# Causal score blocks in two column halves, filler products in TensorE's early gaps, and 224 slots per expert

## The chip, the core and the metric

The kernel runs on one core of one Trainium2 chip. The core has five engines with queues of their own: TensorE (PE in the views; its weight loads are listed apart as PEld), VectorE (DVE), ScalarE (ACT), GpSimd (POOL) and SyncE (SP), which here issues most DMAs. The metric is the device time of one execution in microseconds (us). Matrix products read SBUF and write PSUM, and whatever goes into another product is first copied out of PSUM by ACT or DVE.

## The reference

Inputs q, k, v, a_re, a_im have the shape (4, 8, 768, 48): batch, heads, steps, width. The first half is a linear recurrence with a complex decay, of which the real part is read out:

```python
mag = np.sqrt(a_re * a_re + a_im * a_im)
scale = np.minimum(mag, 0.999) / (mag + 1e-06)
a_re_n, a_im_n = (a_re * scale, a_im * scale)
for t in range(S):
    new_re = ar * S_re - ai * S_im
    new_im = ar * S_im + ai * S_re
    kv = np.einsum('bhd,bhe->bhde', k[:, :, t], v[:, :, t])
    S_re, S_im = (new_re + kv, new_im)
    y[:, :, t] = np.einsum('bhd,bhde->bhe', q[:, :, t], S_re)
```

The result, as 3,072 rows of 384, goes through a mixture of eight experts (widths 384, 1024, 384). A row is computed only if `x @ w_skip > 0`; it goes to the expert with the largest gate logit, and the others are passed through:

```python
for e in range(E):
    mask = e_idx == e
    h = np.maximum(xc[mask] @ w1[e], 0.0)
    y[mask] = gate_w[mask, None] * (h @ w2[e])
out[do_compute] = xc + y
```

With the reference's own inputs 1,500 rows are computed, and the eight experts receive 180, 186, 199, 177, 182, 217, 175 and 184 of them.

## The kernel before, in words

**Units.** Time is cut into six chunks of 128 steps. A unit `u` is one chunk of one batch (all 8 heads), 24 units in all; `c, b = divmod(u, 4)`.

**Attention.** For each unit ACT and DVE make the decay of each step (`gates`), in groups of units because the logarithm, exponential and trigonometric tables of ACT are loaded in turn; running sums over the steps are products with a triangle (`pt`, `pl`). `ready` scales q and k, turns them (`w`), transposes both on TensorE (`tp`, four heads at a time) and copies the transposes to SBUF (`wT`, on ACT). `unit` then makes the scores of four heads at a time (`pa`, line 451): per head one product with 128 key steps as weights (k transposed, 96 rows by 128 columns) and 128 query steps as moving columns. DVE multiplies them with a triangle of ones (`at`, line 457), so that only keys not later than the query remain. `ps` and `T` carry the state, `py` is scores times v plus the state's part. In `py` the weights have 64 columns, and even and odd heads write the lower and the upper 64 partitions of PSUM. `px` makes the gate logits; `route` gives each row a slot of its expert, and an indirect DMA on POOL writes the row there (`xs`).

**Experts.** Each expert has CAP = 256 slots, as two tiles of 128. Numbers are split into a high and a low part in the one-pass format fp32r. Per expert: fetch of the slots (`xg`), six transposes (`tx`, line 862; for the first expert, products `ga` with one-hot rows instead), the split (`xh`, `xl`), 8 groups of 9 products with 128 weight columns and 256 moving columns (`ph`, line 886), relu and split (`hh`, `hl`), 2 by 24 products of 384 moving columns (`po`, lines 907 to 909), scale and add (`og`), and an indirect DMA to the output. If an expert had more rows than slots, a slow branch (`dense`) would follow at the end.

**The order.** `Plan.order` writes out the order of the instructions on each engine ahead of the run: it plays the program through with a cost for each operation (the `us` of `add`), and takes, of what could start within NEAR of the earliest, what has the smallest due time (`at`). The engines then follow that fixed order, and wait where an input is late. The constants at the top (STARTS, LEADS, PULL and others) set the groups and the due times; SHARE names copies that DVE makes in place of ACT.

An f32 product shows in the trace as two instructions (two passes), a transpose and an fp32r product as one.

Of the kernel before, what the change touches and what calls it, by code (L numbers as in the profile page):

```python
# [31 lines left out]
ROOMS = dict(ain=6, tr=5, U=6, cs=2, e=5, qk=4, w0=2, w1=2, wT0=2, wT1=2, vt=3, at=2, st=2, yT=2, row=4, G=1, raw=2, raw2=4,  # L32
             tp=2, pa=2, y=1, g=1, c=2, xa=3, mpt=2, mph=3, mpo=3, xg=2, xh=2, hh=2, og=2)
LEADS = {0: 5.96, 1: 3.48, 2: 2.07, 3: 1.5, 4: 2.5, 5: 2.37, 6: 2.26, 7: 2.47}
SHARE = lambda u: ((0, 1), (1, 1)) if u < 0 else ()
# [7 lines left out]
CAP = 256  # L43
# [4 lines left out]
class Plan:  # L48
# [4 lines left out]

    def __init__(self, rooms):
        self.rooms, self.ops, self.rel = rooms, {}, {}

    def add(self, key, eng, us, at, need=(), take=(), free=()):
        def put(fn):
            need_ = list(need)
            if (key[0], key[1] - 1) + key[2:] in self.ops and key[0][:2] not in ("rt", "ro", "re"):  # L60
                need_.append((None, (key[0], key[1] - 1) + key[2:]))
            self.ops[key] = (eng, us, at, need_, list(take), fn)
            for x in free:
                self.rel.setdefault(x, []).append(key)
        return put

    def order(self):
        end, free, held, out = {}, dict.fromkeys("PAVGS", 0.0), {"xa": [("xa", "z")]}, []
        pipe, warm = 0.0, [-9.0, 0.0]
# [32 lines left out]
        while todo:  # L102
            can = {}
            for key in todo:
                r, e = ready(key), self.ops[key][0][0]
                if r is not None:
                    can.setdefault(e, []).append((max(r, free[e]), self.ops[key][2], key))
# [5 lines left out]
            eng, us, at, need, take, fn = self.ops[key]  # L113
            if len(eng) > 1:
# [3 lines left out]
            else:  # L118
                if e == "P":
                    if s - warm[0] > 3.0:  # L120
                        warm[1] = 0.0
                    if s < COLD or warm[1] < 4.0:
# [12 lines left out]
        assert len(out) == len(self.ops), sorted((k for k in self.ops if k not in end), key=str)[:9]  # L135
# [4 lines left out]
class Kern:  # L140
# [12 lines left out]
    def consts(self, ctx):  # L153
# [57 lines left out]
    def late(self, k):  # L211
# [18 lines left out]
        nc.sync.dma_start(self.xs[k * r:(k + 1) * r].rearrange("(p n) d -> p (n d)", n=B), self.z)  # L230
# [18 lines left out]
    def gates(self, u, k, t, end):  # L249
# [60 lines left out]
        @add(("pt", u), "P", 0.75, t1, [("on" if c else "atan", u)], take=[("c", "pt", u)])  # L310
# [34 lines left out]
        @add(("pl", u), "P", 0.72, t2, [("U", u), ("pt", end - 1)], take=[("c", "pl", u)], free=[("U", u)])  # L345
# [43 lines left out]
    def ready(self, u, t):  # L389
# [15 lines left out]
        for k in range(2):  # L405
# [6 lines left out]
            for hh in range(2):  # L412
                @add(("tp", u, k, hh), "P", 0.455, t, [("w", u, k)], take=[("tp", u, k, hh)], free=[(f"w{k}", u)])
# [19 lines left out]
    def unit(self, u):  # L433
# [7 lines left out]
        @add(("lv", u), "S1", 1.0, t - PULL, take=[("vt", u)])  # L441
        def _():
            vt = X["vt", u] = self.vts[u % len(self.vts)]
            nc.sync.dma_start(vt[:, :, 0:D], self.rows(self.v, c, b))

        for hh in range(2):
            @add(("pa", u, hh), "P", 0.91, t, [("wT", u, k, hh) for k in range(2)], take=[("pa", u, hh)], free=[("wT1", u)])
            def _(hh=hh):
                pa = X["pa", u, hh] = self.ps_at.tile([128, 4, C], F32, name=f"pa_{nm}_{hh}", tag="pa")
                for h in range(hh * 4, hh * 4 + 4):  # L450
                    PE.matmul(pa[:, h % 4], X["wT", u, 1][:, h], X["wT", u, 0][:, h], start=True, stop=True)  # L451

            @add(("at", u, hh), "V", 0.686, t, [("pa", u, hh)], take=[("at", u)], free=[("pa", u, hh)])
            def _(hh=hh):
                if ("at", u) not in X:
                    X["at", u] = self.un.tile([128, H, C], F32, name=f"at_{nm}", tag="at", bufs=self.rooms["at"])
                V.tensor_tensor(X["at", u][:, hh * 4:hh * 4 + 4], X["pa", u, hh],  # L457
                                self.mask.rearrange("p (o t) -> p o t", o=1).to_broadcast([128, 4, C]), ALU.mult)
# [7 lines left out]
        if not late:  # L466
            @add(("ps", u), "P", 1.41, t, [("w", u, 1), ("lv", u)], take=[("g", "ps", u)], free=[("w1", u), ("vt", u)])
            def _():
                ps = X["ps", u] = self.ps_g.tile([96, H, D], F32, name=f"ps_{nm}", tag="g")
                for h in range(H):  # L470
                    PE.matmul(ps[:, h], X["w", u, 1][:, h].rearrange("p k d -> p (k d)"), X["vt", u][:, h, 0:D], start=True, stop=True)
# [9 lines left out]
        for hh in range(2):  # L481
            @add(("py", u, hh), "P", 0.97 if c else 0.48, t,
                 [("at", u, hh), ("lv", u)] + ([("Sb", u), ("wT", u, 0, hh)] if c else []),
                 take=[("y", u)], free=[("at", u), ("vt", u), ("wT0", u)] + [("st", u)] * (c > 0))
            def _(hh=hh):
# [3 lines left out]
                vt, at, qT, py = X["vt", u], X["at", u], X["wT", u, 0], X["py"]  # L489
# [14 lines left out]
        @add(("px", u), "P", 0.9, t, [("yT", u), ("wg", 0)], take=[bank], free=[("yT", u)])  # L504
# [43 lines left out]
    def early(self):  # L548
# [3 lines left out]
        nx = CAP // 128 * DM  # L552
        self.xe = m[:, 0:nx].rearrange("p (t d) -> p t d", d=DM)
        self.ohx = [o[:, b * CAP:(b + 1) * CAP] for b in range(B - 1)] + [m[:, nx:nx + CAP]]
        self.nc.sync.dma_start(self.xe, self.xs[0:CAP, 0:DM].rearrange("(t p) d -> p t d", p=128))
# [138 lines left out]
    def attention(self):  # L694
        with ExitStack() as ctx:
# [5 lines left out]
            self.ps_tp, self.ps_at = P("ps_tp", 2, space=PSUM), P("ps_at", 2, space=PSUM)  # L701
# [3 lines left out]
            self.vts = [pers.tile([128, H, 64], F32, name=f"vt{i}") for i in range(self.rooms["vt"])]  # L705
            self.sts = [pers.tile([96, H, 64], F32, name=f"st{i}") for i in range(self.rooms["st"])]
            for t in self.vts + self.sts:
# [109 lines left out]
    def experts(self):  # L817
# [6 lines left out]
        ks = lambda k: slice(k * 128, (k + 1) * 128)  # L824
        wTs = [("wT", u, k, hh) for k in range(2) for hh in range(2)]
        self.weights(1, n - 1.5, 0.15, [("w", u, 1)])

        def pts(e, t):
            if ("pts", e, t) not in X:
                X["pts", e, t] = self.pt_.tile([128, KD, 128], F32, name=f"pt_{e}_{t}", tag="pt")  # L830
            return X["pts", e, t]

        for b in (0, 1, 2, -1, 3):
# [4 lines left out]
            def _(b=b):  # L838
                for t in range(2):
                    for k in range(KD):  # L840
                        l, r = (self.xe[:, t, ks(k)], self.ident) if b < 0 else (self.xa[:, b, ks(k)], self.ohx[b][:, ks(t)])
                        PE.matmul(pts(0, t)[:, k], l, r, start=(b == 0 and k == 0), stop=True, skip_group_check=True)

        for e in range(E):
            te = T0 + TE * e

            @add(("xg", e), "S1", 1.1, te - 0.9, [("px", u)] + [(f"re{b}", 8) for b in range(B)], take=[("xg", e)])
            def _(e=e):
                xg = X["xg", e] = self.xp.tile([128, 2, XW], F32, name=f"xg_{e}", tag="xg")
                nc.sync.dma_start(xg, self.xs[e * CAP:(e + 1) * CAP].rearrange("(t p) d -> p t d", p=128))  # L850

            @add(("idx", e), "G", 0.2, te - 0.8, [("xg", e)])
            def _(e=e):
                X["idx", e] = self.xp.tile([128, 2], I32, name=f"idx_{e}", tag="idx")
                G.tensor_copy(X["idx", e], X["xg", e][:, :, DM])

            for t in range(2):
                if e:
                    @add(("tx", e, t), "P", 0.34, te - 0.8, [("xg", e)], take=[("mpt", e, t)])
                    def _(e=e, t=t):  # L860
                        for k in range(KD):
                            PE.transpose(pts(e, t)[:, k], X["xg", e][:, t, ks(k)], self.ident)

                @add(("xh", e, t), "A", 0.482, te - 0.75, [("tx", e, t) if e else ("ga", 3)], take=[("xh", e)])
                def _(e=e, t=t):
                    if ("xh", e) not in X:
                        X["xh", e], X["xl", e] = [self.xp.tile([128, KD, CAP], F32R, name=f"{a}_{e}", tag=a) for a in ("xh", "xl")]
                    A.copy(X["xh", e][:, :, ks(t)], pts(e, t))

                @add(("xl", e, t), "V", 0.553, te - 0.75, [("xh", e, t)], free=[("mpt", e, t)])  # L870
                def _(e=e, t=t):
                    V.tensor_tensor(X["xl", e][:, :, ks(t)], pts(e, t), X["xh", e][:, :, ks(t)], ALU.subtract)  # L872

            for j in range(NF):
                @add(("ph", e, j), "P", 1.08, te + j * 0.11,
# [12 lines left out]
                @add(("hh", e, j), "A", 0.381, te + j * 0.11, [("ph", e, j)], take=[("hh", e)])  # L888
# [5 lines left out]
                @add(("hl", e, j), "V", 0.418, te + j * 0.11, [("hh", e, j)], free=[("mph", e, j)])  # L894
# [3 lines left out]
            for t in range(2):  # L898
                for j in range(NF):
                    @add(("po", e, t, j), "P", 0.52, te + 0.95 + (t * NF + j) * 0.053,  # L900
                         [("hl", e, j), ("wl", e, KD + j // 2)] + [(None, ("po", e, t, j - 1))] * (j > 0) + [("px", u)] * (e == 0),
                         take=[("mpo", e, t)], free=[("hh", e)])
                    def _(e=e, t=t, j=j):
                        if j == 0:
                            X["po", e, t] = self.po_.tile([128, DM], F32, name=f"po_{e}_{t}", tag="po")
# [246 lines left out]
```

## Time and profile before

| | |
|---|---|
| median of 3 runs | 425.59 us (425.2 to 426.17) |
| the profiled execution | 426.13 us, its span 424.4 us |
| TensorE busy | 388.5 us (92%), 3,236 instructions |
| DVE busy | 319.3 us (75%) |
| ACT busy | 283.9 us (67%) |
| POOL busy | 56.6 us (13%) |
| DMA moved | 65.55 MB |
| mean granted TensorE clock | 0.979 |

The span goes from the first to the last instruction; the time of an execution has some 1.7 us more around it. A busy TensorE is not one at its peak: successive products overlap, so the distance between their starts is what one costs, not its duration. The granted clock is 1.00 at 2.4 GHz and 0.50 at 1.2 GHz.

### The profile page before, as it was taken

The page shows a single profiled execution, that of the slowest core. Times are in us where ns is not written, and L with a number is a line of the kernel's source. Part 1 is how long each engine was busy: PE and PEld are TensorE (multiplying, and loading weights), DVE is VectorE, ACT ScalarE, POOL GpSimd, SP SyncE. Part 2 cuts the span into 40 slices and gives each one's busy share as a digit, 9 for nine tenths or more (in the row PEclk, how much of TensorE's full clock was granted, in tenths as well). Part 3 has the DMA queues.
Part 4 walks back from the last instruction along what each step waited for, and adds up shares of the span by engine and source line. Part 5 has one row for each costly group of instructions (what it writes and reads, how often), then busy time and mean ns, then how long its engine had stood idle before and what let it go on. Part 6 is the DMA issues. An engine that isn't in the chain of part 4 may idle for free. (4 is left out here: it accounts for less than half of the span.)

```text
span 424.4 us, 8790 instructions
## 1 busy us (share of the span) xinstructions
PE 388.5 (92%) x3236; PEld 346.3 (82%) x3236; DVE 319.3 (75%) x722; ACT 283.9 (67%) x550; POOL 56.6 (13%) x94
## 2 busy tenths in 40 slices
PE   0569999999999999999999988899999999999992
PEld 0248689769868987997878977799999999999992
DVE  4469799979999978987997998877666676656220
ACT  5798998889798879849898654554454655446020
POOL 7000000014005003001300121101011010111101
PEclk9967999999999999999999999999999999999998
DMA  9999929986983892444423765586665766662001
GB/s 158 184 148 171 161 58 177 366 150 142 158 168 81 139 194 54 97 80 112 101 48 119 206 213 195 159 294 223 206 236 179 233 177 230 227 192 80 27 1 33
DMA packets 148049, 65.55 MB, mean 154 GB/s; under 512 B 129323, under 2 KB 143407, under 8 KB 148000
## 3 DMA queue, kind: packets, MB, share of 16 engines
q1 hardware_dynamic: 145440, 60.29, 60.7%
q0 software_dynamic: 2560, 4.63, 3.0%
q8 instruction: 28, 0.46, 0.5%
q14 instruction: 21, 0.17, 0.1%
HBM read 52.33 MB, written 15.77 MB: 160 GB/s over the span
## 5 line engine op out<-in xcount | busy, mean ns | idle before, releaser
L810 ACT CAST h<-r 128x768 fp32r<-128x768 f32 (+1 forms) x56 | 50.8, 926 | 38.5 <-issue 19.8
L815 DVE TENSOR_TENSOR l<-r,h 128x768 fp32r<-128x768 f32 (+1 forms) x56 | 58.9, 1069 | 7.8 <-ACT h L810 7.2
L558 POOL DMA_INDIRECT xs<-xa,sl x24 | 28.9, 1206 | 231.3 <-ACT tr L242 85.0
L418 PE MATMUL tp<-ident,w 128*96 128x128 f32 x384 | 55.0, 284 | 3.0 <-ACT wT L427 1.2
L886 PE MATMUL ph<-xh,h 128*128 128x256 f32 x192 | 54.6, 288 | 1.1 <-DVE hl L896 0.8
L418 PEld LDWEIGHTS tp<-ident,w 128*96 128x96 f32 x384 | 43.1, 131 | 14.6 <-issue 4.4
L427 ACT COPY wT<-tp 96x512 f32<-96x512 f32 x96 | 52.1, 580 | 2.8 <-PE tp L418 2.6
L886 PE MATMUL ph<-xh,l 128*128 128x256 f32 x192 | 53.6, 283 | 0.0
L451 PE MATMUL pa<-wT,wT 96*128 96x128 f32 x384 | 52.4, 284 | 0.1
L886 PE MATMUL ph<-xl,h 128*128 128x256 f32 x192 | 51.8, 283 | 0.3 <-DVE xl L872 0.3
L892 ACT ACTIVATE hh<-ph 128x256 fp32r<-128x256 f32 x64 | 24.3, 383 | 40.1 <-PE ph L886 40.1
L451 PEld LDWEIGHTS pa<-wT,wT 96*128 96x128 f32 x384 | 47.9, 197 | 2.3 <-issue 0.7
L410 DVE TENSOR_TENSOR w<-qk,cs 128x768 f32<-128x768 f32 x48 | 45.3, 951 | 0.2
L907 PE MATMUL po<-h,hh 128*128 128x384 f32 x128 | 43.6, 340 | 0.0
L896 DVE SCALAR_TENSOR_TENSOR hl<-ph,hh 128x256 fp32r<-128x256 f32 x64 | 26.2, 419 | 22.4 <-ACT hh L892 22.4
L909 PE MATMUL po<-h,hl 128*128 128x384 f32 x128 | 43.0, 336 | 0.0
L908 PE MATMUL po<-l,hh 128*128 128x384 f32 x128 | 43.0, 336 | 0.0
L492 PE MATMUL py<-at,vt 128*64 128x128 f32 x384 | 37.8, 282 | 1.6 <-DVE at L457 1.2
L886 PEld LDWEIGHTS ph<-xh,h 128*128 128x128 f32 x192 | 36.7, 191 | 2.2 <-DVE hl L896 1.0
L457 DVE TENSOR_TENSOR at<-pa,mask 128x512 f32<-128x512 f32 x48 | 32.6, 684 | 7.8 <-PE pa L451 7.7
L886 PEld LDWEIGHTS ph<-xh,l 128*128 128x128 f32 x192 | 36.6, 191 | 0.0
L313 PE MATMUL pt<-tr,turns 128*128 128x384 f32 x48 | 22.1, 563 | 15.3 <-ACT tr L242 14.9
(158 smaller groups left out, 774.1 us busy)
## 6 DMA issues: line engine op xcount, KB each, us to landing
r<-in_moe_w_dram SPq DMA_DIRECT2D x24, 512.0 KB, 4.7
r<-in_moe_w_dram SPq DMA_DIRECT2D x32, 384.0 KB, 4.0
ain<-in_a_re_dram SPq DMA_DIRECT2D x24, 192.0 KB, 4.3
ain<-in_a_im_dram SPq DMA_DIRECT2D x24, 192.0 KB, 4.5
qk<-in_q_dram SPq DMA_DIRECT2D x24, 192.0 KB, 3.9
qk<-in_k_dram SPq DMA_DIRECT2D x24, 192.0 KB, 4.2
vt<-in_v_dram SPq DMA_DIRECT2D x24, 192.0 KB, 3.3
out_dram<-xa SPq DMA_DIRECT2D x5, 768.0 KB, 5.2
```

What stands on the lines that cost most here:

```text
L410: V.tensor_tensor(n, X["qk", u][:, k].unsqueeze(2).to_broadcast([128, H, 2, D]), X["cs", c][:, b], ALU.mult)
L418: nc.tensor.transpose(tp[:, h], n[:, hh * 4 + h].rearrange("p k d -> p (k d)"), self.ident)
L427: (V.tensor_copy if onV else A.copy)(X["wT", u, k][:, hh * 4:hh * 4 + 4], X["tp", u, k, hh])
L451: PE.matmul(pa[:, h % 4], X["wT", u, 1][:, h], X["wT", u, 0][:, h], start=True, stop=True)
L457: V.tensor_tensor(X["at", u][:, hh * 4:hh * 4 + 4], X["pa", u, hh], self.mask.rearrange("p (o t) -> p o t", o=1).to_broadcast([128, 4, C]) ...
L492: PE.matmul(py[j * 64:j * 64 + 64, hp], vt[:, 2 * hp + j], at[:, 2 * hp + j], start=True, stop=(c == 0))
L810: nc.scalar.copy(X["W", e, n][0][:, ks], X["raw", e, i])
L815: nc.vector.tensor_tensor(lo[:, ks], X["raw", e, i], hi[:, ks], ALU.subtract)
L886: PE.matmul(ph, w[:, k, ks(j)], x[:, k], start=(i == 0), stop=(i == len(terms) - 1))
L907: PE.matmul(po, hh[:, j, ks(t)], w2h[:, j], start=(j == 0), stop=False)
L908: PE.matmul(po, hh[:, j, ks(t)], w2l[:, j], start=False, stop=False)
L909: PE.matmul(po, hl[:, j, ks(t)], w2h[:, j], start=False, stop=(j == NF - 1))
```

## The change

1. **Scores.** For each head the block of late queries (64 to 127) with late keys and the block of all queries with early keys are made apart, with 64 weight columns each; late keys with early queries are left out. The two blocks go to the two halves of the PSUM partitions, swapped for odd heads. The two PSUM tiles are kept and cleared once. `masks` holds the triangle and a swapped triangle, and v is loaded a second time for the odd heads with its step halves swapped (`vs`, two more DMAs per unit).
2. **Fillers.** Where the played-through plan shows TensorE idle after 9.0 us and before the first `py`, products of `turns` with itself are put in, one for each 0.23 us less 0.25 us.
3. **Slots.** CAP is 224, in two tiles of 112 rows; `xg` has three buffers, not two.
4. **Plan.** Costs, due times and constants are new; a change between {`py`, `pa`} and other TensorE work counts 0.1 us; DVE makes two of the four `wT` copies for the first two units.

```diff
-STARTS = [0, 3, 7, 11, 15, 18, 21]
-AHEAD, TRIG, READY, PULL = 3.0, 0.63, 1.05, 3.44
-NEAR, COLD = 0.1, 33.0
-WAFTER, WGAP, CHECK = 0.75, 0.21, 2
+STARTS = [0, 3, 7, 11, 14, 18, 21]
+AHEAD, TRIG, READY, PULL = 3.0, 1.48, 1.28, 2.95
+NEAR, COLD = 0, 33.0
+WAFTER, WGAP, CHECK = 0.41, 0.29, 3
+FETCH = 1.69
+FILL = 9.0
...
-LEADS = {0: 5.96, 1: 3.48, 2: 2.07, 3: 1.5, 4: 2.5, 5: 2.37, 6: 2.26, 7: 2.47}
-SHARE = lambda u: ((0, 1), (1, 1)) if u < 0 else ()
+LEADS = {0: 7.67, 1: 3.67, 2: 2.09, 3: 2.19, 4: 3.21, 5: 1.9, 6: 1.57, 7: 2.34}
+SHARE = lambda u: ((0, 1), (1, 1)) if u < 2 else ()
...
-CAP = 256
+CAP = 224
+HALF = CAP // 2
...
+    HALVES = ("py", "pa")
...
-                    can.setdefault(e, []).append((max(r, free[e]), self.ops[key][2], key))
+                    can.setdefault(e, []).append((max(r, free[e]) + 0.1 * (e == "P" and mode != (key[0] in self.HALVES)), self.ops[key][2], key))
...
+            n = int((s - max(free["P"], FILL) - 0.25) / 0.23)
+            if e == "P" and n > 0 and ("py", 0, 0) not in end:
+                out.append((max(free["P"], FILL), ("fill", len(out)), lambda n=n: self.fill(n)))
+                warm = [s, 9.0]
...
+        self.masks = cst.tile([128, 2, 128], F32, name="masks")
+        g.tensor_copy(self.masks[:, 0], self.mask)
+        m = self.masks[:, 1]
+        g.memset(m[0:64, 0:64], 0.0)
+        g.memset(m[64:128, 64:128], 1.0)
+        g.tensor_copy(m[0:64, 64:128], self.mask[0:64, 0:64])
+        g.tensor_copy(m[64:128, 0:64], self.mask[64:128, 64:128])
...
-        @add(("lv", u), "S1", 1.0, t - PULL, take=[("vt", u)])
+        @add(("lv", u), "S3", 1.6, t - PULL, take=[("vt", u)])
...
+            for lo, hi in ((slice(0, 64), slice(64, C)), (slice(64, C), slice(0, 64))):
+                nc.sync.dma_start(vs[hi, :, 0:D], v[lo, 1::2])
...
-            @add(("pa", u, hh), "P", 0.91, t, [("wT", u, k, hh) for k in range(2)], take=[("pa", u, hh)], free=[("wT1", u)])
+            @add(("pa", u, hh), "P", 0.62, t, [("wT", u, k, hh) for k in range(2)], take=[("pa", u, hh)], free=[("wT1", u)])
             def _(hh=hh):
-                pa = X["pa", u, hh] = self.ps_at.tile([128, 4, C], F32, name=f"pa_{nm}_{hh}", tag="pa")
-                for h in range(hh * 4, hh * 4 + 4):
-                    PE.matmul(pa[:, h % 4], X["wT", u, 1][:, h], X["wT", u, 0][:, h], start=True, stop=True)
+                pa = X["pa", u, hh] = self.pas[hh]
+                q, k = X["wT", u, 0], X["wT", u, 1]
+                late, early, low, high = slice(64, C), slice(0, 64), slice(0, 64), slice(64, C)
+                for i, p, ts in ((1, high, early), (1, low, late), (0, high, late), (3, low, late),
+                                 (2, high, late), (0, low, early), (3, high, early), (2, low, early)):
+                    h = hh * 4 + i
+                    t0 = 0 if ts == early else 64
+                    PE.matmul(pa[p, i, t0:], k[:, h, ts], q[:, h, t0:], start=True, stop=True)
...
-                        PE.matmul(py[j * 64:j * 64 + 64, hp], vt[:, 2 * hp + j], at[:, 2 * hp + j], start=True, stop=(c == 0))
+                        PE.matmul(py[j * 64:j * 64 + 64, hp], vs[:, hp] if j else vt[:, 2 * hp], at[:, 2 * hp + j], start=True, stop=(c == 0))
...
+            self.pas = [self.ps_at.tile([128, 4, C], F32, name=f"pa{i}") for i in range(2)]
+            for x in self.pas:
+                nc.vector.memset(x, 0.0)
...
+            self.plan.fill = self.idle
...
+    def idle(self, n):
+
+        if "warm" not in self.x:
+            self.x["warm"] = self.ps_y.tile([128, H // 2, C], F32, name="warm", tag="py")
+        for i in range(n):
+            self.nc.tensor.matmul(self.x["warm"][:, 0], self.turns, self.turns, start=True, stop=True)
...
-            @add(("xg", e), "S1", 1.1, te - 0.9, [("px", u)] + [(f"re{b}", 8) for b in range(B)], take=[("xg", e)])
+            @add(("xg", e), "S1", 1.1, te - FETCH, [("px", u)] + [(f"re{b}", 8) for b in range(B)], take=[("xg", e)])
...
-                @add(("ph", e, j), "P", 1.08, te + j * 0.11,
+                @add(("ph", e, j), "P", 1.01, te + j * 0.11,
```

The new table SHIFT adds between -1.13 and 1.35 units to the due times of 36 kinds of operations; the other lines of the diff replace 128 by HALF in shapes and adjust costs.

## Rows read from the trace of the kernel before

**Rows 1.** Windows by stage: length; PE, PEld, DVE, ACT, POOL busy; clock; DMA share, GB/s.

```profile
24.40:38.00 13.60, 12.64 (x55) 10.47 (x56) 12.97 (x26) 11.57 (x24) 0.00 (x0) 0.50 0.97 162
...
60.00:255.00 195.00, 189.49 (x1858) 162.80 (x1856) 176.73 (x430) 160.15 (x318) 27.91 (x26) 1.00 0.63 143
255.00:283.00 28.00, 24.91 (x226) 22.99 (x227) 22.15 (x85) 14.07 (x27) 3.75 (x6) 1.00 0.66 216
283.00:416.00 133.00, 131.89 (x921) 130.19 (x920) 79.55 (x128) 59.50 (x112) 15.92 (x21) 1.00 0.51 166
```

**Rows 2.** Waits of TensorE from 40 to 260 us: total, times, longest.

```profile
PE py L492 <- DVE at L457: 1.2, 4, 0.4
```

**Rows 3.** Timeline of TensorE from 150 to 215 us: start, length, engine, instruction, count.

```profile
152.49 1.04 PE L509 MATMUL px<-wg,yT 128*128 128x105 f32 x8
...
155.66 1.14 PE L451 MATMUL pa<-wT,wT 96*128 96x128 f32 x8
...
158.40 0.44 PE L492 MATMUL py<-at,vt 128*64 128x128 f32 x4
...
165.78 1.06 PE L451 MATMUL pa<-wT,wT 96*128 96x128 f32 x8
...
203.95 1.97 PE L451 MATMUL pa<-wT,wT 96*128 96x128 f32 x16
...
208.67 0.44 PE L492 MATMUL py<-at,vt 128*64 128x128 f32 x4
```

**Rows 4.** Groups by line and shape: count, busy us, mean ns of one, idle before.

```profile
L451 PE MATMUL pa<-wT,wT 96*128 96x128 f32 x384 | 52.4, 284 | 0.1
...
L451 PEld LDWEIGHTS pa<-wT,wT 96*128 96x128 f32 x384 | 47.9, 197 | 2.3 <-issue 0.7 <-ACT wT L427 0.5 <-ACT h L810 0.2
...
L492 PEld LDWEIGHTS py<-at,vt 128*64 128x64 f32 x384 | 22.0, 135 | 7.5 <-DVE at L457 3.1 <-issue 2.2 <-PE px L509 0.5
```

**Rows 5.** Timeline of TensorE from 39.6 to 42.5 us.

```profile
39.72 1.48 PE L471 MATMUL ps<-vt,w 128*96 128x48 f32 x16
41.13 1.09 PE L492 MATMUL py<-at,vt 128*64 128x128 f32 x16
42.15 0.59 PE L313 MATMUL pt<-tr,turns 128*128 128x384 f32 x1
```

**Rows 6.** Windows of 20 us, columns as in Rows 1: two of the ten.

```profile
120.00:140.00 20.00, 19.30 (x182) 16.16 (x180) 19.09 (x45) 18.30 (x39) 5.53 (x5) 1.00 0.52 124
...
180.00:200.00 20.00, 19.77 (x192) 16.74 (x189) 15.48 (x46) 13.85 (x31) 0.04 (x1) 1.00 0.43 100
```

**Rows 7.** The tile vt: issues on SP, ns min/median/max.

```profile
L444 SPq DMA_DIRECT2D vt<-in_v_dram x24: 367/454/2447, 11.9 to 239.6; - x24
```

**Rows 8.** Timeline of TensorE up to 60 us, early part.

```profile
14.86 4.58 PE L313 MATMUL pt<-tr,turns 128*128 128x384 f32 x6 [14.86 <-ACT tr L242]
...
24.91 1.65 PE L348 MATMUL pl<-U,mask 128*128 128x384 f32 x2 [3.04 <-ACT e L242]
...
33.45 3.78 PE L451 MATMUL pa<-wT,wT 96*128 96x128 f32 x16
```

**Rows 9.** Timeline of ACT up to 62 us, two of its waits.

```profile
6.26 0.61 ACT L242 ACTIVATE tr<-ain,col 128x384 f32<-128x384 f32 x1 [1.33 <-POOL twice L159]
...
16.52 0.49 ACT L317 ACTIVATE tr<-pt 128x384 f32<-128x384 f32 x1 [0.97 <-PE pt L313]
```

**Rows 10.** Timeline of POOL up to 30 us, clearing of the v tiles' pads.

```profile
3.60 0.47 POOL L708 MEMSET vt<- 128x128 f32 x3
```

**Rows 11.** Timeline of TensorE from 376 us, with the experts' products.

```profile
376.30 0.34 PE L907 MATMUL po<-h,hh 128*128 128x384 f32 x1
...
376.82 0.34 PE L907 MATMUL po<-h,hh 128*128 128x384 f32 x1
...
383.11 0.28 PE L886 MATMUL ph<-xh,h 128*128 128x256 f32 x1
...
384.19 0.28 PE L886 MATMUL ph<-xh,h 128*128 128x256 f32 x1
```

**Rows 12.** Waits of TensorE from 255 to 425 us: total, times, longest.

```profile
PE pt L862 <- DMA xg<-xs: 1.7, 4, 0.6
```

More of the change, by code (lines that the diff above doesn't have):

```diff
@@ L61, in put @@
                 need_.append((None, (key[0], key[1] - 1) + key[2:]))
-            self.ops[key] = (eng, us, at, need_, list(take), fn)
+            self.ops[key] = (eng, us, at + SHIFT.get(key[0], 0.0), need_, list(take), fn)
             for x in free:
@@ L68, in order @@
         end, free, held, out = {}, dict.fromkeys("PAVGS", 0.0), {"xa": [("xa", "z")]}, []
-        pipe, warm = 0.0, [-9.0, 0.0]
+        pipe, warm, mode = 0.0, [-9.0, 0.0], False
         left, users, base, todo = {}, {}, {}, set()
@@ L119, in order @@
                 if e == "P":
+                    mode = key[0] in self.HALVES
                     if s - warm[0] > 3.0:
                         warm[1] = 0.0
-                    if s < COLD or warm[1] < 4.0:
+                    if s < FILL + 6.0 or warm[1] < 4.0:
                         us *= 2
@@ L134, in order @@
                     start(x)
-        assert len(out) == len(self.ops), sorted((k for k in self.ops if k not in end), key=str)[:9]
+        assert len(end) == len(self.ops), sorted((k for k in self.ops if k not in end), key=str)[:9]
         self.end = end
@@ L343, in _ @@
             self.table(X["cs", c][:, b, :, 0], X["tr", u][:, 0], AF.Sin, scale=-2 * math.pi, bias=self.hpi)
-        @add(("pl", u), "P", 0.72, t2, [("U", u), ("pt", end - 1)], take=[("c", "pl", u)], free=[("U", u)])
+        @add(("pl", u), "P", 0.73, t2, [("U", u), ("pt", end - 1)], take=[("c", "pl", u)], free=[("U", u)])
         def _():
@@ L412, in ready @@
             for hh in range(2):
-                @add(("tp", u, k, hh), "P", 0.455, t, [("w", u, k)], take=[("tp", u, k, hh)], free=[(f"w{k}", u)])
+                @add(("tp", u, k, hh), "P", 0.468, t, [("w", u, k)], take=[("tp", u, k, hh)], free=[(f"w{k}", u)])
                 def _(k=k, hh=hh):
@@ L456, in _ @@
                     X["at", u] = self.un.tile([128, H, C], F32, name=f"at_{nm}", tag="at", bufs=self.rooms["at"])
-                V.tensor_tensor(X["at", u][:, hh * 4:hh * 4 + 4], X["pa", u, hh],
-                                self.mask.rearrange("p (o t) -> p o t", o=1).to_broadcast([128, 4, C]), ALU.mult)
+                two = lambda x: x.rearrange("p (a j) t -> p a j t", j=2)
+                V.tensor_tensor(two(X["at", u][:, hh * 4:hh * 4 + 4]), two(X["pa", u, hh]),
+                                self.masks.unsqueeze(1).to_broadcast([128, 2, 2, C]), ALU.mult)
         if c > 0:
@@ L502, in unit @@
         bank = ("c" if late else "g", "px", u)
-        @add(("px", u), "P", 0.9, t, [("yT", u), ("wg", 0)], take=[bank], free=[("yT", u)])
+        @add(("px", u), "P", 0.925, t, [("yT", u), ("wg", 0)], take=[bank], free=[("yT", u)])
         def _():
@@ L704, in attention @@
             self.rooms = dict(ROOMS)
-            self.vts = [pers.tile([128, H, 64], F32, name=f"vt{i}") for i in range(self.rooms["vt"])]
+            self.vts = [[pers.tile([128, n, 64], F32, name=f"{a}{i}") for a, n in (("vt", H), ("vs", H // 2))] for i in range(self.rooms["vt"])]
+            self.pas = [self.ps_at.tile([128, 4, C], F32, name=f"pa{i}") for i in range(2)]
+            for x in self.pas:
+                nc.vector.memset(x, 0.0)
             self.sts = [pers.tile([96, H, 64], F32, name=f"st{i}") for i in range(self.rooms["st"])]
-            for t in self.vts + self.sts:
+            for t in [x for p in self.vts for x in p] + self.sts:
                 nc.gpsimd.memset(t[:, :, D:64], 0.0)
```

63 lines of the change are left out of this document (33 added, 30 removed).

## The prediction

> **What bounds the kernel now.** I read the stages first. From 60 to 255 us TensorE is busy 189.5 of 195 us, DVE 176.7, ACT 160.2; from 283 to 416 us TensorE 131.9 of 133, DVE only 79.6 [rows 1]. So TensorE sets the time almost from 40 us on, but in the attention DVE stands close behind it. The waits agree: the costliest wait of TensorE between 40 and 260 us sums to 1.2 us [rows 2]. Only the start is different. From 24.4 to 38 us the granted clock is 0.50, TensorE is busy 12.6 of 13.6 us, and DVE 13.0 [rows 1]. The last question is what one product costs when TensorE is full; that comes from the distance between starts in the timeline, not from durations.
>
> **Scores.** A run of 16 passes of `pa` takes 1.97 us [rows 3], and one of them 0.28 [rows 4], so passes start (1.97 - 0.28)/15 = 0.113 us apart, and a half unit (8 passes) costs 0.90. For `py`, which has 64 weight columns like the new scores, 16 passes take 1.09 us [rows 5]: as eight pairs that is (1.09 - 0.28)/7 = 0.116 per pair. The two column halves work side by side, their weight loads too. A new half unit has in each column half two products of 128 columns and two of 64. In passes of 0.11 us that is 2 x 0.22 + 2 x 0.11 = 0.66 us if the halves run freely beside each other, and 1.32 if one waits for the other throughout. Between them lies strict starting in order: as written, the third product waits for its column half while the other is idle for 0.11, which makes 0.77. No row pairs products of different length. I take 0.66, since `py`'s pairs lose nothing [rows 5]: 48 x (0.90 - 0.66) = 11.5 us less; the bounds are 6.2 less and 20 more.
>
> Against this stands the change of mode. The last pass of `ps` starts at 39.72 + 1.48 - 0.25 = 40.95 us and the `pt` behind `py` at 42.15 [rows 5]. Of these 1.20 us, 0.08 is a step of `ps` ((1.48 - 0.25)/15) and 8 x 0.11 the pairs; 0.24 us is the way into and out of the split array. From 155.7 to 208.7 us I count 10 separate runs of `pa` and 8 of `py` [rows 3], over about six units. If every run of `pa` stayed alone, 10/6 x 24 = 40 new visits would cost 9.6 us. The new planner charges 0.1 us for a switch and so prefers to stay; I take one new visit per unit, 24 x 0.24 = 5.8 us (bounds 10 and 40 visits, 2.4 and 9.6 us). Net: 5.7 us less on TensorE.
>
> Not all of it shows, because DVE is the next bound: it is busy 19.1 of 20 us in one window but 15.5 in another [rows 6], and `at` still covers all 128 by 512. I count three quarters, **4.3 us** (between 8 less and 4 more). The second load of v costs nothing here: SP issues one load of v in 0.45 us [rows 7], so 48 more are 22 us on SP's queue, behind which later loads stand; the bytes are 24 x 96 KB = 2.3 MB, in a stage where DMA is busy 0.63 [rows 1]. What hides them is the lead of about three units; without it each unit would start 0.9 us later. `py` must now wait for three loads rather than one, which land in the same lead.
>
> **Start.** The first products run at half pace: six passes of `pt` take 4.58 us, and 16 of `pa` 3.78 [rows 8], against 1.97 later [rows 3]. ACT waits 0.97 us for the first `pt` [rows 9]. If fillers have the clock up by then, that wait and the following ones lose about 1.0 us. From 24.4 to 38 us, at most half of 12.6 us is to be had on TensorE; but DVE has 0.6 us free there [rows 1], and it now takes four `wT` copies as well. I take 2.5 us less. On the other side, ACT waits 1.33 us for constants from POOL at 6.26 us [rows 9], and POOL gets five operations for `masks` and three more pads (0.47/3 = 0.16 each [rows 10]) ahead of them: 8 x 0.16 = 1.3 us, of which I count 1.0. Fillers that run at half pace last about 0.43 us, not 0.23 (two passes, each half of the pace above); in the gap of 3.04 us before 24.91 [rows 8], 12 of them would end 2 us late. Start in total **2.5 us less**, between 6 less and 3 more.
>
> **Experts.** Nine products of `ph` lie between 383.11 and 384.19 us, 0.120 each; three of `po` take 0.52, 0.173 each [rows 11]. Per column that is 0.053/128 = 0.41 ns, so 32 columns fewer would give 0.107. But weights have 128 columns still. `px`, with 105 moving columns, starts a pass every (1.04 - 0.28)/7 = 0.109 us, and `pa` with 128 one every 0.113 [rows 3]: with 128 weight columns the distance does not follow the moving columns below about 0.11. I take 0.112: 8 x 72 x (0.120 - 0.112) = 4.6 us less, bounds 0 and 7.6. `po` keeps its 384 moving columns; fewer weight columns don't matter there. The Trainium skill (TensorE: Matmul & The Clock Gate, section LDWEIGHTS) gives a load as its columns over 1.2 GHz, so an estimate by that page is 0.107 for 128 columns and a term of 7.5 us; the load's durations, 197 ns for 128 columns and 135 for 64 [rows 4], show the dependence on columns and not this figure. TensorE waits 1.7 us for `xg` in four experts [rows 12]; the third buffer and the earlier fetch should take away 1.5. Shorter transposes give 0.3. Together **6.4 us less**. The scatter at the end has the same row length and costs nothing new. No expert has more than 217 rows, so 224 slots hold them.
>
> **Sum.** 426.1 - 4.3 - 2.5 - 6.4 = 412.9 us for an execution like the profiled one, which lies 0.5 above the median of the runs; so 412.4 us.
>
> **Rivals.** (a) Products start strictly in order and every run of `pa` stays alone. Attention then gains 6.2 and pays 9.6: 425.6 + 3.4 - 2.5 - 6.4 = 420.1 us. For it: ten separate runs [rows 3]; against it: the planner's new charge. The Trainium skill (TensorE: Matmul & The Clock Gate, Part 3, "The mechanism") says that products start and end in program order, and `py`'s pairs of equal length [rows 5] can't show what that costs with unequal ones; the rule would give this rival's term of 0.77 us for a half.
>
> (b) DVE is the bound as soon as TensorE is shorter. Attention gains 1 us, the start loses 1 (four copies more on a full DVE): 425.6 - 1 + 1 - 6.4 = 419.2 us. For it: 19.1 of 20 us [rows 6]; against it: 15.5 in another window.
>
> (c) Slower: blocks of unequal length don't overlap at all. A half unit costs 1.32 instead of 0.90, so 48 x 0.42 + 5.8 = 26 us more, against 8.9 less elsewhere: 442.7 us. It decides from about 0.96 us per half unit upwards ((8.9 - 5.8)/48 above 0.90). Against it: the pairs of `py`.
>
> (d) The planner needs few switches, the start gains 5 and the columns alone set `ph` (8 with the rest): 425.6 - 9 - 5 - 8 = 403.6 us.
>
> (e) The clock does not rise although the fillers run: the start gains nothing and pays POOL's 1.0 and a late filler's 2.0, 425.6 - 4.3 + 3 - 6.4 = 417.9 us. The row of 0.50 at a busy TensorE [rows 1] speaks for it, the pace of `pa` from 60 us on, at 1.00, against it.
>
> (f) Below 256 columns fp32r loses its one-pass rate. No row has such a product. At f32's 0.22 for 128 columns, 224 would take 0.39, and 576 x 0.27 = 153 us more make 579 us.
>
> **Chances.** Forecast 0.40; (a) 0.14; (b) 0.12; (c) 0.06; (d) 0.16; (e) 0.07; (f) 0.02; an order that stalls somewhere I can't name 0.03, slower or the same. The likeliest case gives 412.4 us. The range 401 to 421.5 holds the forecast, (a), (b), (e) and most of (d), and leaves out (c), (f) and the tails. This kernel's measurement tells 0.2% from no change. Faster 0.87, same 0.03, slower 0.10.
>
> **What would show it.** In the new trace, a run of `pa` in the middle should last about 0.66 us per half to the next run's start plus 0.24 for its visit; 0.9 or more makes the scores' step wrong. Visits to the split mode should be about 60. The window from 24.4 to 38 us should show a clock of 1.00, and ACT's first wait on POOL should be near 2.5 us. Starts of `ph` should lie 0.112 us apart, and the wait of `pt` for `xg` be gone. Between 60 and 240 us DVE should be over 93% busy; if it is and TensorE falls to 90%, (b) holds. I am wrong if the stage from 283 us on is not some 6 us shorter, or if the attention's end moves by less than 3 us.

## The result and the profile after

The changed kernel takes 413.76 us (median of four runs, 412.21 to 415.26), the kernel before 425.74 beside it. The ratio is 0.9719, with a 95% interval of 0.9695 to 0.9744. Forecast were 412.4 us, so the total is right. Its parts are less so. All ratios here go by fast runs alone; of the experiments, narrow columns of `ph` and the operation on GpSimd also had two slow runs each, which lift their medians. In the traces the span goes from 424.4 to 412.5 us:

| stretch | before | after | change | forecast |
|---|---|---|---|---|
| start and attention, up to the first `ph` | 270.9 | 266.8 | -4.1 | -6.8 |
| experts, first `ph` to last `po` | 145.7 | 138.2 | -7.5 | -6.4 |
| behind the last `po` | 7.8 | 7.5 | -0.3 | 0 |

The table rests on the first and last starts of `ph` and `po`, in before and then in after (count, ns min/median/max, first and last start):

```profile
L886 PE MATMUL ph<-xh,h x192: 277/283/388, 270.9 to 408.1; 128*128 128x256 f32 x192
L909 PE MATMUL po<-h,hl x128: 332/336/345, 280.5 to 416.6; 128*128 128x384 f32 x128
```

```profile
L925 PE MATMUL ph<-xh,h x192: 261/274/373, 266.8 to 396.5; 128*128 128x224 f32 x192
L948 PE MATMUL po<-h,hl x128: 332/337/342, 276.3 to 405.0; 128*112 128x384 f32 x128
```

The windows by stage, which answer to [rows 1]; one window from 14 to 21 us is added, and the columns are those of [rows 1].

```profile
14.00:21.00 7.00, 5.79 (x13) 3.41 (x14) 2.65 (x6) 4.98 (x12) 0.00 (x0) 0.59 1.44 187
24.40:38.00 13.60, 11.76 (x114) 10.13 (x113) 12.54 (x27) 11.86 (x23) 0.00 (x0) 1.00 0.72 137
60.00:255.00 195.00, 185.32 (x2272) 158.62 (x2269) 174.71 (x429) 158.65 (x316) 29.92 (x26) 1.00 0.68 155
...
283.00:416.00 133.00, 121.45 (x890) 119.94 (x888) 74.33 (x126) 55.36 (x108) 19.68 (x21) 0.98 0.53 159
```

The clock is 1.00 from 24.4 to 38 us, as hoped, but 0.59 a little earlier. In the attention TensorE now leaves 9.7 of 195 us free; before it left 5.5. So it is less of a bound than it was.

The timeline of TensorE at the first products (to be held against [rows 8]) and at a run of `pa` in the attention (against [rows 3]):

```profile
2.74 6.79 PE L753 MATMUL warm<-turns 128*128 128x128 f32 x44 [2.74 <-POOL turns L170]
14.99 2.93 PE L331 MATMUL pt<-tr,turns 128*128 128x384 f32 x4 [5.47 <-ACT tr L260]
...
57.31 1.55 PE L477 MATMUL pa<-wT,wT 96*64 96x64 f32 x32
58.87 1.14 PE L536 MATMUL px<-wg,yT 128*128 128x105 f32 x8
```

The first fillers start as soon as `turns` is there, at 2.74 us, and are over at 9.5. Then TensorE stands for 5.47 us, and four passes of `pt` take 2.93 us again, the pace of [rows 8]. So this batch warms nothing. In the attention both halves of a unit's `pa` run together, right behind `py`. Their 16 products, 32 passes, start within 1.55 - 0.27 = 1.28 us; with one step of 0.11 that is 1.39 us, or 0.70 per half. Forecast were 0.66, strict order would give 0.77, and before it was 0.90.

TensorE's waits from 40 to 260 us, the answer to [rows 2]: total, times, longest.

```profile
PE px L536 <- DVE cand L633: 2.0, 2, 1.4
PE pt L881 <- DVE ohx L677: 1.9, 1, 1.9
PE pr L673 <- DVE oh L688: 1.3, 1, 1.3
PE tp L436 <- DVE w L428: 1.1, 2, 0.8
PE px L536 <- ACT wT L445: 1.1, 2, 0.8
```

In the first place of [rows 2] stood a wait of 1.2 us; four of these five are for DVE. The wait of `pt` for `xg` [rows 12] is in no list any more.

### The profile page after: what moved, and what is told of

It reads as the page before. It is cut to its first block, busy times and chain, and to the rows that moved or that the text cites. A ratio compares the mean times of both kernels' runs of the same rounds, so it can differ in the third digit from the quotient of the medians.

```text
span 412.5 us, 9865 instructions
## 1 busy us (share of the span) xinstructions
PE 379.5 (92%) x3742; PEld 341.0 (83%) x3742; DVE 317.3 (77%) x728; ACT 278.7 (68%) x546; POOL 64.3 (16%) x102
## 5 line engine op out<-in xcount | busy, mean ns | idle before, releaser
L848 ACT CAST h<-r 128x768 fp32r<-128x768 f32 (+1 forms) x56 | 51.1, 925 | 39.6 <-PE po L948 19.3
L925 PE MATMUL ph<-xh,h 128*128 128x224 f32 x192 | 52.7, 279 | 1.7 <-DVE hl L935 1.4
L925 PE MATMUL ph<-xh,l 128*128 128x224 f32 x192 | 51.9, 274 | 0.0
L925 PE MATMUL ph<-xl,h 128*128 128x224 f32 x192 | 50.1, 275 | 0.0
L946 PE MATMUL po<-h,hh 128*112 128x384 f32 x128 | 43.6, 341 | 0.0
L947 PE MATMUL po<-l,hh 128*112 128x384 f32 x128 | 43.1, 337 | 0.0
L948 PE MATMUL po<-h,hl 128*112 128x384 f32 x128 | 43.1, 337 | 0.0
L477 PE MATMUL pa<-wT,wT 96*64 96x128 f32 (+1 forms) x768 | 38.7, 250 | 1.1 <-issue 0.6
L477 PEld LDWEIGHTS pa<-wT,wT 96*64 96x64 f32 x768 | 34.1, 137 | 2.4 <-issue 1.5
L519 PE MATMUL py<-at,vs 128*64 128x128 f32 x192 | 36.1, 278 | 0.0
L925 PEld LDWEIGHTS ph<-xl,h 128*128 128x128 f32 x192 | 35.5, 192 | 0.0
```

The costliest lines, as they stand in the source:

```text
L477: PE.matmul(pa[p, i, t0:], k[:, h, ts], q[:, h, t0:], start=True, stop=True)
L519: PE.matmul(py[j * 64:j * 64 + 64, hp], vs[:, hp] if j else vt[:, 2 * hp], at[:, 2 * hp + j], start=True, stop=(c == 0))
L848: nc.scalar.copy(X["W", e, n][0][:, ks], X["raw", e, i])
L925: PE.matmul(ph, w[:, k, ks(j)], x[:, k], start=(i == 0), stop=(i == len(terms) - 1))
L946: PE.matmul(po, hh[:, j, ts(t)], w2h[:, j], start=(j == 0), stop=False)
L947: PE.matmul(po, hh[:, j, ts(t)], w2l[:, j], start=False, stop=False)
```

## Experiments

**The new kernel once more.** No edit; it is the yardstick, on the same chip, for undivided scores, less for DVE and less for TensorE. 

> The changed kernel unchanged, as the measure for the three beside it on the same chip. 412 to 415 us.

Measured 413.78 us (413.21 to 414.52), ratio 0.9718 (0.9678 to 0.9758).

**Without the fillers.**

```diff
-        for i in range(n):
+        for i in range(0):
```

> The changed kernel in the same order, without the filler products themselves. If the fillers earn the 2.5 us that the prediction gave the start, this takes 1 to 4 us longer than the changed kernel (415 to 418 us), with the granted clock at 0.50 somewhere between 22 and 38 us. If DVE covers TensorE there, the time stays within 1 us of 413.8 although the clock falls.

Measured 415.3 us, ratio 0.9756 (0.9721 to 0.9791). Windows of this kernel:

```profile
14.00:21.00 7.00, 5.41 (x9) 2.27 (x10) 2.92 (x6) 5.22 (x12) 0.00 (x0) 1.00 1.42 187
24.40:38.00 13.60, 9.65 (x52) 7.22 (x54) 11.56 (x25) 10.54 (x23) 0.00 (x0) 0.55 0.78 146
```

The clock falls to 0.55 from 24.4 to 38 us. In the first window the row says 1.00, although six passes of `pt` have the old pace there:

```profile
15.17 4.19 PE L331 MATMUL pt<-tr,turns 128*128 128x384 f32 x6 [15.17 <-ACT tr L260]
```

The first unit's `yT` comes 2.1 us later than in after, and the first `ph` 1.6 us later (268.4). The fillers raise the clock and are worth 1.5 to 2 us, a little under the 2.5 that the prediction gave the start; in the total it is 1.5 us, with overlapping intervals.

**The first fillers late.** They read unit 0's `U`, so they can't start at 2.74 us, and there are 13 of them.

```diff
-        for i in range(n):
-            self.nc.tensor.matmul(self.x["warm"][:, 0], self.turns, self.turns, start=True, stop=True)
+        first = "pt0" not in self.x
+        self.x["pt0"] = True
+        moving = self.x["U", 0].rearrange("p h d -> p (h d)")[:, 0:128] if first else self.turns
+        for i in range(13 if first else n):
+            self.nc.tensor.matmul(self.x["warm"][:, 0], self.turns, moving, start=True, stop=True)
```

> In the changed kernel the first batch of 22 fillers ran from 2.7 to 9.5 us, and the first pt came at 15.0 at half pace. Here the first batch is 13 products that read U of unit 0 and so start near 9.7 us. If the pt chain on ACT sets the start, ACT's waits for pt fall from 2.0 to about 0.8 us in sum and the kernel gains about 1 us (412.8). If DVE sets it from 25 us on, or the clock is not up at 15 us, nothing changes.

Measured 412.04 us (411.18 to 412.27), ratio 0.9677 (0.9648 to 0.9707). By the medians it is the fastest kernel here that does the whole work, 1.7 us under the changed one; the two intervals overlap a little. Its window from 14 to 21 us:

```profile
14.00:21.00 7.00, 6.39 (x26) 4.33 (x26) 2.83 (x6) 6.09 (x14) 0.00 (x0) 1.00 1.45 187
```

And its timeline of TensorE:

```profile
9.81 5.85 PE L756 MATMUL warm<-U,turns 128*128 128x128 f32 x26 [9.81 <-POOL zrow L236]
15.49 1.46 PE L331 MATMUL pt<-tr,turns 128*128 128x384 f32 x4
```

The fillers now end where `pt` begins. The clock is 1.00 instead of 0.59, and four passes take 1.46 us instead of 2.93. The first unit's `yT` comes 1.0 us earlier, the first `ph` 3.3 us earlier (263.5); where the rest of that arises stands under less for TensorE.

**Order of the blocks.** Once blocks of equal length side by side, once all blocks of the upper half first.

```diff
-                for i, p, ts in ((1, high, early), (1, low, late), (0, high, late), (3, low, late),
-                                 (2, high, late), (0, low, early), (3, high, early), (2, low, early)):
+# pairs
+                for i, p, ts in ((1, high, early), (0, low, early), (3, high, early), (2, low, early),
+                                 (0, high, late), (1, low, late), (2, high, late), (3, low, late)):
+# apart
+                for i, p, ts in ((1, high, early), (0, high, late), (2, high, late), (3, high, early),
+                                 (1, low, late), (3, low, late), (0, low, early), (2, low, early)):
```

> The eight blocks of a half in another order, so that blocks of one length stand side by side (early with early, late with late). A half takes 0.70 us in the changed kernel; strict starting in order would allow 0.66 here. Then TensorE has 48 x 0.04 = 1.9 us less to do. If TensorE is still the bound of the attention, 1 to 2 us less time (412 to 413); if not, no change. If the queues of the two column halves are free of each other, a half stays at 0.70 or falls alike and the order doesn't matter.

Measured 412.16 us (411.29 to 412.87), ratio 0.9683 (0.9652 to 0.9714). In the timeline of this kernel the run is hardly shorter than after's 1.55 us:

```profile
56.90 1.51 PE L477 MATMUL pa<-wT,wT 96*64 96x128 f32 x32
```

So unequal neighbours cost about 0.04 us per unit, 24 x 0.04 = 1.0 us in all. Why the kernel is 1.6 us faster than after, and its first `ph` 2.4 us earlier (264.4), is known only in part (see the stop under less for TensorE); the intervals overlap.

> The four blocks of the upper column half first, then the four of the lower. If products start strictly in order, the two halves of the array run one after the other: about 1.3 us per half unit instead of 0.70, 48 x 0.6 = 29 us more on TensorE, 435 to 443 us. If the two halves have queues of their own that look ahead, a half stays near 0.70 and the time near 414.

Measured 414.31 us, ratio 0.9733 (0.9694 to 0.9771). The same run in its timeline:

```profile
57.33 1.90 PE L477 MATMUL pa<-wT,wT 96*64 96x128 f32 x32
```

The tile `pa` in the same run up to 57.77 us (count, ns min/median/max, first and last start, shapes):

```profile
L477 PE MATMUL pa<-wT,wT x7: 217/222/274, 57.3 to 57.7; 96*64 96x64 f32 x5, 96*64 96x128 f32 x2
```

The run takes 0.35 us more, not the 1.3 of two halves that don't overlap. And as written, the order is two passes of 128 columns, four of 64, two of 128, and only then the lower half's. Of the first seven starts five are of 64 columns; the upper half has only four before its second pair of 128. So at least one pass of the free half started ahead of that pair. For the total: 24 x 0.35 = 8.4 us more on TensorE cost about 0.5 us against after, with overlapping intervals.

**Undivided scores in the new order.** The rest of the change stays.

```diff
-                for i, p, ts in ((1, high, early), ...
...
-                    PE.matmul(pa[p, i, t0:], k[:, h, ts], q[:, h, t0:], start=True, stop=True)
+                for i in range(4):
...
+                    PE.matmul(pa[:, i], k[:, h], q[:, h], start=True, stop=True)
...
```

> The changed kernel in its own order, but with undivided scores: one product of 128 by 128 per head, plain triangle, odd heads with plain v. A half costs 0.90 us again instead of 0.64 to 0.70, some 48 x 0.22 = 11 us more on TensorE. If TensorE is the bound of the attention, nearly all of it shows: 421 to 424 us. If DVE and the fixed order bound it, a quarter or less: 414 to 417 us.

Measured 415.28 us (414.18 to 415.92), ratio 0.9757 (0.9717 to 0.9797): 1.5 us over the new kernel once more (413.78), with overlapping intervals. The first `ph` starts 0.6 us later. The window of the attention in this kernel:

```profile
60.00:255.00 195.00, 190.59 (x1923) 167.26 (x1924) 175.89 (x430) 158.54 (x316) 26.14 (x26) 1.00 0.67 154
```

TensorE is busy 5.3 us longer there than in after (by the distance between starts it has 48 x 0.20 = 9.6 us more to do), and the time hardly answers.

**Less for DVE, less for TensorE.** In the first, two of four heads of each half get no masked scores, and `py` reads the first two in their place. In the second, half of the score blocks are left out, at 0.70 us a half 24 x 0.70 = 16.8 us less for TensorE.

```diff
# dve_light
-                V.tensor_tensor(two(X["at", u][:, hh * 4:hh * 4 + 4]), two(X["pa", u, hh]), ...
+                V.tensor_tensor(X["at", u][:, hh * 4:hh * 4 + 2], X["pa", u, hh][:, 0:2], self.masks, ALU.mult)
...
-                        PE.matmul(py[...], ..., at[:, 2 * hp + j], start=True, stop=(c == 0))
+                        PE.matmul(py[...], ..., at[:, hh * 4 + j], start=True, stop=(c == 0))
# pe_light
+                for i, p, ts in ((1, high, early), (1, low, late), (0, high, late), (0, low, early)):
```

> VectorE masks only two of each four heads' scores (128 by 256 instead of 128 by 512), and the products with v read those two twice, so the output is not the reference's. DVE has 48 x 0.3 = 14 us less to do, TensorE the same. If DVE bounds the attention, 6 to 10 us less than the changed kernel (404 to 408); if TensorE does, under 2 us less.

Measured 408.52 us (408.21 to 409.66), ratio 0.9599 (0.956 to 0.9639): 5.3 us less than after. The first `ph` starts 5.1 us earlier (261.7). The tile `at` on DVE, in after, with TensorE's waits for it (total, times), and then in this kernel (count, ns min/median/max):

```profile
L484 DVE TENSOR_TENSOR at<-pa,masks x48: 672/680/693, 46.3 to 252.5; 128x512 f32<-128x512 f32 x48
...
  PEld py L519: 1.1, 3
  PE py L519: 0.5, 1
```

```profile
L484 DVE TENSOR_TENSOR at<-pa,masks x48: 405/415/425, 46.3 to 247.4; 128x256 f32<-128x256 f32 x48
```

So DVE had 48 x (0.680 - 0.415) = 12.7 us less to do. The shorter `at` also shortens each unit's way from `pa` to `py`, but TensorE waits only 1.6 us in all for `at` in after, so that explains little of the 5.3 us.

> The scores of two of each four heads are left out (four of eight blocks), so the output is not the reference's. TensorE has 48 x 0.33 = 16 us less to do, DVE the same. If TensorE bounds the attention, 8 to 14 us less than the changed kernel (400 to 406); if DVE and the order do, under 3 us less.

Measured 2779.51 us. With other scores more rows went to one expert than it has slots, and the slow branch for that case ran at the end. Up to the experts the trace still tells: the first `ph` starts at 265.8 us, 1.0 earlier than in after. Its window of the attention:

```profile
60.00:255.00 195.00, 173.53 (x1935) 147.21 (x1933) 175.47 (x431) 158.88 (x317) 33.60 (x26) 0.99 0.68 156
```

And TensorE's largest waits from 40 to 260 us:

```profile
PE px L535 <- ACT yT L526: 5.0, 8, 1.3
PE px L535 <- DVE cand L632: 2.8, 3, 1.5
PE tp L436 <- DVE w L428: 2.5, 3, 1.7
```

TensorE's 16.8 us become waits for ACT and DVE and give one; DVE's 12.7 us give five. DVE is the nearer bound.

Even that one us has another reason. In after, TensorE stops once within a run of `pa`, and the profile names nothing that it waited for:

```profile
100.10 1.30 PE L477 MATMUL pa<-wT,wT 96*64 96x64 f32 x19
101.71 0.82 PE L477 MATMUL pa<-wT,wT 96*64 96x64 f32 x13 [0.30 <-issue]
```

The new kernel's second trace has this stop too; the kernels with less for TensorE, less for DVE, late fillers and blocks side by side have none there. With less for TensorE the sixth unit's `yT` comes no earlier than in after, the eleventh's, behind the stop, 0.9 us earlier; with late fillers it is 1.0 and 2.4 us. With less for DVE the lead keeps growing, from 1.1 us at the sixth to 5.1 at the last. What causes the stop is open, and differences of 1 us between these kernels can't be put down to the work that was taken away.

**Columns of `ph`.** Seven of nine products have 128 moving columns, so the hidden layer of the other 96 slots is not summed in full.

```diff
-                        PE.matmul(ph, w[:, k, ks(j)], x[:, k], ...
+                        m = CAP if i == 0 or i == len(terms) - 1 else 128
+                        PE.matmul(ph[:, 0:m], w[:, k, ks(j)], x[:, k, 0:m], ...
```

> The changed kernel with seven of the nine products of each ph group over 128 moving columns instead of 224 (the rest of the columns gets no such terms, so the output is not the reference's). If the 128 weight columns set the distance, ph stays at 0.112 us and the time at 413 to 414. If the moving columns do, a narrow product takes 0.066 us and the experts lose 448 x 0.04 = 18 us: 395 us.

Measured 417.06 us (412.84 to 420.16), ratio 0.971 (0.966 to 0.976), which is that of the changed kernel: no gain. The starts in its timeline say why.

```profile
362.88 0.23 PE L926 MATMUL ph<-xl,h 128*128 128x128 f32 x1
362.95 0.28 PE L926 MATMUL ph<-xh,l 128*128 128x128 f32 x1
363.06 0.27 PE L926 MATMUL ph<-xh,h 128*128 128x128 f32 x1
...
363.51 0.27 PE L926 MATMUL ph<-xl,h 128*128 128x128 f32 x1
...
363.88 0.23 PE L926 MATMUL ph<-xl,h 128*128 128x128 f32 x1
```

From 363.06 on, four steps take 0.45 us, 0.112 each; the first step, 0.07, is shorter and those at the change of width are longer. Nine steps, from 362.88 to 363.88, take 1.00 us, as with 224 columns in after:

```profile
354.60 0.27 PE L925 MATMUL ph<-xh,h 128*128 128x224 f32 x1
...
355.04 0.28 PE L925 MATMUL ph<-xl,h 128*128 128x224 f32 x1
...
355.60 0.28 PE L925 MATMUL ph<-xh,h 128*128 128x224 f32 x1
```

So the moving columns do not hold the distance. That the 128 weight columns do is argued from [rows 5], where `ps` with 96 weight columns starts every 0.08 us; no run changed the weight columns of `ph`.

**The slots alone, in the kernel before.** Shapes of 224 slots and the cost of `ph` in the plan; two `xg` buffers, the old fetch and the old constants stay.

```diff
-CAP = 256
+CAP = 224
+HALF = CAP // 2
...
-                @add(("ph", e, j), "P", 1.08, te + j * 0.11,
+                @add(("ph", e, j), "P", 1.01, te + j * 0.11,
```

> The kernel before with 224 slots per expert in two tiles of 112 and nothing else (old constants, two buffers for the fetch). The prediction gave ph 4.6 us and the transposes 0.3; the waits for the fetch (1.7 us) stay. 420.0 to 421.5 us against 425.6; if weight loads don't hold ph at 0.112 us, 417 to 418.

Measured 431.07 us, ratio 1.0121 (1.0076 to 1.0166): slower than before. First `ph` 270.1, last `po` 423.1 us: 153.0 us for the experts, against 145.7 before and 138.2 after. TensorE's largest wait from 255 us on:

```profile
PE pt L864 <- DMA xg<-xs: 9.4, 6, 2.0
```

The tile `xg` in the same kernel, its issues on SP and their landing:

```profile
L852 SPq DMA_DIRECT2D xg<-xs x8: 332/371/424, 272.9 to 390.4; - x8
...
DMA to landing us min/median/max: 5.9/7.5/8.0
```

Two windows of the experts:

```profile
320.00:340.00 20.00, 18.89 (x126) 18.44 (x126) 11.51 (x18) 8.20 (x16) 2.51 (x3) 0.91 0.60 182
...
380.00:400.00 20.00, 19.86 (x135) 19.45 (x134) 11.31 (x21) 8.04 (x17) 2.75 (x4) 0.91 0.33 97
```

The same row of after, where the last issue is at 358.0 us and nobody on TensorE waits for one:

```profile
L889 SPq DMA_DIRECT2D xg<-xs x8: 327/372/458, 270.0 to 358.0; - x8
```

Each `ph` is shorter here too (273 ns in the median, 283 before), but a load of `xg` takes 7.5 us to land (before 6.1), starts only when a buffer is free (the last is issued at 390.37 us, behind the `og` that ends at 390.30), and TensorE waits 9.4 us for six of them; after such waits the clock is 0.91 in two windows. So with two buffers and the old fetch narrower slots don't gain at all, and the third buffer and the earlier fetch are worth more than the 1.5 us that I gave them. How much more is not shown: the old due times stayed too, and no run adds the buffer alone.

**The blocks alone, in the kernel before.** Masks, second load of v, blocks, the charge for a switch and the new costs in the plan; the old constants stay.

```diff
-                    PE.matmul(pa[:, h % 4], X["wT", u, 1][:, h], X["wT", u, 0][:, h], start=True, stop=True)
+                    PE.matmul(pa[p, i, t0:], k[:, h, ts], q[:, h, t0:], start=True, stop=True)
...
```

> The kernel before with the score blocks, their masks, the second load of v and the planner's charge for a switch, but with the old constants, slots and no fillers. TensorE has some 10 us less to do. If TensorE bounds the attention of the kernel before, 5 to 10 us less (416 to 421); if DVE and the order already bound it, 0 to 2 us less (424 to 426), or more where the old due times fit the new order badly.

Measured 434.91 us, ratio 1.0195 (1.0165 to 1.0226). The experts take 145.8 us, as before; the loss lies ahead of them, with the first `ph` at 281.5 us. Two windows from where most of it arises:

```profile
200.00:220.00 20.00, 15.62 (x180) 13.47 (x177) 19.52 (x47) 15.16 (x31) 6.37 (x5) 0.97 0.46 90
220.00:240.00 20.00, 19.97 (x196) 15.72 (x195) 14.05 (x23) 16.07 (x30) 0.00 (x0) 0.86 0.24 69
```

And TensorE's two largest waits in them:

```profile
PE px L527 <- DVE T L495: 2.3, 2, 1.5
PE pt L322 <- DVE tr L317: 0.9, 1, 0.9
```

First DVE is full (19.5 of 20) and TensorE idles 4.4 us, then the clock falls to 0.86 and DVE idles. Visits to the split mode rise from 38 to 53, so by the prediction's 0.24 us each they take back 3.6 us. With the old due times, then, shorter scores lose 9 us. That the unfitted order does it is the likely reading; the second load of v and the masks changed along with it, and no run parts them.

**One DVE operation to GpSimd.** The decay of the state (`st`), in the kernel with late fillers and in its order.

```diff
-                V.tensor_tensor(X["Sb", u][:, :, 0:D], X["T", b], ...
+                nc.gpsimd.tensor_tensor(X["Sb", u][:, :, 0:D], X["T", b], ...
```

> The late first fillers, and the state's decay (st, 20 times 96 x 384) made on GpSimd instead of VectorE in the same order. DVE has 20 x 0.55 = 11 us less to do. If DVE bounds the attention, by the slope of the lighter masks (14 us less work gave 5.3) 4 us less than the late fillers alone: 408 us. If GpSimd is slow or its work comes late, no gain: 412 or more.

Measured 426.61 us, ratio 1.0 (0.9971 to 1.003), some 14 us more than the kernel it is made from. Its timelines of POOL and of TensorE:

```profile
96.58 1.20 POOL L585 DMA_INDIRECT xs<-xa,sl  x1 [26.93 <-DMA vt<-in_v_dram]
97.81 0.85 POOL L491 TENSOR_TENSOR st<-T,Fall 96x384 f32<-96x384 f32 x1
...
99.30 1.04 PE L498 MATMUL ps<-vt,w 128*96 128x48 f32 x5 [10.17 <-DVE T L504]
```

One operation takes 0.855 us on GpSimd and 0.548 on DVE. But the harm is the place in the queue: a scatter stands ahead of the decay and waits until 96.58 us, so `T` and then `ps` wait 10.2 us. The try says nothing on how DVE would do with less work in an order made for it.

## Why the prediction was right in sum and wrong in parts

The step that failed is "Not all of it shows, because DVE is the next bound ... I count three quarters". Both factors were off. TensorE saves more than the 5.7 us: 48 x (0.90 - 0.70) = 9.6 for the blocks, and visits to the split mode, counted in the timelines, fell from 38 to 29 instead of rising by 24, because the new order mostly puts both halves of `pa` behind a `py`; 9 x 0.24 = 2.2 more, 11.8 in all. Of the blocks' 9.6 us 0.6 to 1.5 shows (undivided scores in the same order), and half of the score blocks less gives 1.0. Lightening DVE by 12.7 gives 5.1. So in the attention the mechanism of rival (b) held, though not its 419.2 us, and although its sign did not come: DVE is busy 164.3 of 180 us from 60 to 240, 91% and not over 93, TensorE 171.8, 95% and not 90. Neither is full; with an order written out beforehand each engine stands now and then for the other, and the one nearer the chain is found by taking work away, not by shares.

The start's 2.5 us were near: 1.5 to 2 from the fillers. My step for POOL's masks failed, since ACT no longer waits for POOL in the new order, and so did "that wait and the following ones lose about 1.0 us": ACT waits 2.0 us for `pt`, because the first fillers came too early. Moved to where `pt` starts they bring 1.0 us more at the first unit's `yT`, and ACT waits 1.3. ACT's row of after, over the first 24 us:

```profile
ACT tr L335 <- PE pt L331: 2.0, 3, 0.9
```

Of the 4.1 us up to the first `ph`, fillers (1.6) and blocks (0.6) leave some 1.9. That this is the new order is only a remainder; no run has the order alone. The two parts tried alone show what an unfitted order costs.

The experts' term was right in kind and 1.1 us small. `ph` starts 0.112 us apart as forecast, 4.6 us; the 1.7 us of `xg` waits are gone (0.2 more than forecast), and transposes went from 0.109 to 0.096 us a step, 0.5 us. The last 0.7 I can't assign. The term for the third buffer and the earlier fetch was right only as against before; with narrow slots in the old plan these waits are 9.4 us.

That the sum came so near is in part luck: start and attention gave 2.7 us less than forecast, experts and tail 1.4 more, and some 1.9 us of the attention's gain stand where I had put the score blocks, and are not shown to be theirs.

Rival (a) is out: a half costs 0.70 and not 0.77, and in the experiment with the upper blocks first the free half ran ahead. The Trainium skill (TensorE: Matmul & The Clock Gate, Part 3, "The mechanism") has products start in program order; this trace differs, with five starts of 64 columns ahead of the third of 128, one more than program order allows, and the measurement decides. Rivals (c) and (f) are out by the same row and by `ph` at 0.112. Rival (d) had the few switches right, but neither its attention nor its `ph`; (e) is out, as the clock was 1.00 from 24.4 to 38 us. The Trainium skill (TensorE: Matmul & The Clock Gate, section LDWEIGHTS) would give an estimate of 0.107 us for 128 weight columns; the measured distance is 0.112, with 128 moving columns and with 224.

## What to carry to other kernels

Before an operation on a full engine is made shorter, make the next engine lighter in an experiment and see which one the time follows: here 16.8 us less on TensorE gave about one, and 12.7 us less on DVE gave five. A shortened stage may need its loads earlier and its order made anew; both parts of this change, put alone into the old plan, made the kernel slower. Fillers that keep a clock up belong right ahead of the work they serve, which takes an input that arrives at that time.

## What the runs showed that I had not expected

- Products on one column half of the split array start ahead of earlier ones on the other: 1.90 us for a run of two half units, each of which would take 1.32 if the column halves never overlapped.
- With 128 moving columns or with 224, products of `ph` with 128 weight columns start 0.112 us apart in the mean of nine.
- Loads of `xg` with fewer bytes (338 KB each instead of 386) took longer to land, 7.5 us instead of 6.1 in the median; why is open.
- The first fillers warmed nothing: between 14 and 21 us, behind 5.47 us of idle TensorE, the clock was 0.59, and `pt` had its old pace; fillers that ended where `pt` began gave 1.00 and half the time.
